# Keeping later chunks' q in block order through the MLP, with the stores putting rows in place and a new list of steps

**Chip, cores, metric.** One core of one Trainium2 chip. The metric is the device time of one execution in microseconds (us); lower is better.

## The reference, cut

```python
# attention: gated linear recurrence, B=4, H=8, S=768, D=48
state = alpha[:, :, t, :, None] * state + einsum('bhd,bhe->bhde', k[:, :, t], v[:, :, t])
y[:, :, t] = einsum('bhd,bhde->bhe', q[:, :, t], state)
# bridge to (3072, 384), then the MLP, d_ff = 2048
h = x @ w_in
g = h * np.clip(h + 3.0, 0.0, 6.0) / 6.0
out = g @ w_out
```

## The kernel before

24 chunks of 128 tokens (six for each batch) go through the recurrence; pairs of chunks ("groups") go through the MLP. The first six chunks are transposed by TensorE. From chunk 6 on (`FIRST = 6`) alpha, k and q are loaded in a layout from which VectorE's 32x32 block transposes make the columns; each transpose writes with a stride of four fp32, so that tokens come out in natural order:

```python
def by_blocks(to, name, j):
    nc.vector.transpose(out=to.rearrange("r p (u v) -> r p v u", v=V),
                        in_=quads[name, j % NQ][:, :, :, 0:BLK])
```

k must also be had with tokens in the partitions. From chunk 6 on it is turned by VectorE (`kt`), written to DRAM by four SyncE DMAs (`kw`), and read back by one (`kr`); TensorE uses it for the state update (`u`):

```python
def read_k(j):                                   # step kr
    kb_t[j] = wk.tile([C, NP, C], FP, tag="kb", name="kb")
    nc.sync.dma_start(out=kb_t[j].rearrange("s p r -> s (p r)"),
                      in_=far_t.pop(j).rearrange("s v p o c -> v s (p o c)"))
# ... cut: update(j), step u, multiplies kb_t[j] by v ...
def store2(g, i):                                # step O, on ScalarE's queue
    row, col = PLACES[i]
    j = G * g + row
    nc.scalar.dma_start(out=out[j * C : (j + 1) * C, col * HD : (col + 1) * HD],
                        in_=oh_t.pop((g, i)))
```

Loads, `kw` and `kr` all stand in SyncE's one queue, in order. The order on every engine is set by hand: a long list of words (`kw.12 ... lq.12 ... kr.12 ... u.12`), each word one step of one chunk or group. The framework adds the semaphores. (A semaphore marks that a piece of work is done; what depends on that work waits for it.) In the compiled program all DMAs of SyncE and ScalarE share eight completion semaphores in rotation, and a DMA of SyncE waits until the one that used its semaphore before has landed.

## Time and profile before

| | before |
|---|---|
| device time, first set of three | 568.94 us (568.49 to 569.09) |
| span of the profiled run | 564.6 us |
| first product of the second group (L692) | 113.2 us |
| first product of the last group | 543.2 us |
| last matmul | 561.2 us |

The prediction below shows the main lines. What TensorE waited for (total, times, longest, in us), and what SyncE's queue waited for, taken from the list of waits:

```profile
PE u_ps L410 <- DMA kb<-far: 2.1, 2, 1.1
PE tk_ps L288 <- DMA rings<-in_k_dram: 2.0, 2, 1.9
...
SPq L267 <- DMA out_dram<-oh: 27.7, 13, 4.6
```

The first line is the state update waiting for k's read-back. The last is SyncE, whose loads (L267) stood 13 times and for 27.7 us behind stores (`out_dram<-oh`) that they have no data in common with.

### The profile page before, as it was taken

The page shows a single profiled execution, that of the slowest core. Times are in us where ns is not written, and L with a number is a line of the kernel's source. Part 1 is how long each engine was busy: PE and PEld are TensorE (multiplying, and loading weights), DVE is VectorE, ACT ScalarE, POOL GpSimd, SP SyncE. Part 2 cuts the span into 40 slices and gives each one's busy share as a digit, 9 for nine tenths or more (in the row PEclk, how much of TensorE's full clock was granted, in tenths as well). Part 3 has the DMA queues.
Part 4 walks back from the last instruction along what each step waited for, and adds up shares of the span by engine and source line. Part 5 has one row for each costly group of instructions (what it writes and reads, how often), then busy time and mean ns, then how long its engine had stood idle before and what let it go on. Part 6 is the DMA issues. An engine that isn't in the chain of part 4 may idle for free.

```text
span 564.6 us, 12762 instructions
## 1 busy us (share of the span) xinstructions
PE 553.4 (98%) x5236; PEld 513.2 (91%) x5236; DVE 470.0 (83%) x798; ACT 196.4 (35%) x348; POOL 56.0 (10%) x70
## 2 busy tenths in 40 slices
PE   8899999999899999999999999999999999999997
PEld 7688987599799989999999999999999999999997
DVE  7866997999899999998998978976999967754580
ACT  1457664112332332322422422432521422432420
POOL 2333435200001000100000000000000000000000
PEclk9979999999999999999999999999999999999999
DMA  9999677103533636264264353153154340000000
GB/s 147 188 186 168 186 230 196 52 16 63 139 90 87 145 71 155 54 139 90 60 148 107 77 121 85 20 146 78 45 129 94 83 122 8 1 22 8 1 30 21
DMA packets 121272, 53.73 MB, mean 95 GB/s; under 512 B 80638, under 2 KB 114174, under 8 KB 121214
## 3 DMA queue, kind: packets, MB, share of 16 engines
q1 hardware_dynamic: 114588, 48.19, 40.8%
q10 hardware_dynamic: 6624, 4.72, 2.5%
q8 instruction: 41, 0.67, 0.5%
q14 instruction: 19, 0.14, 0.1%
HBM read 44.24 MB, written 8.65 MB: 94 GB/s over the span
## 4 chain that ended last, share of the span: by engine, by line
PE 89%; DMA 6%; DVE 2%; SPq 1%; issue 0%; ACT 0%; DVEq 0%; ACTq 0%
PE m_ps L692 35%; PE m_ps L592 29%; PE m_ps L471 6%; PE sc_ps L346 4%; PE m_ps L509 4%; PE y_ps L440 4%; DMA rings<-in_k_dram 3%; PE y_ps L450 2%; PE m_ps L482 2%; DMA t<-in_v_dram 2%; PE u_ps L410 2%; DMA kb<-far 1%; PE tk_ps L288 1%; DMA far<-kq 1%; PE m_ps L524 0%
## 5 line engine op out<-in xcount | busy, mean ns | idle before, releaser
L692 PE MATMUL m_ps<-w,g_sb 128*128 128x192 f32 x704 | 121.2, 328 | 0.0
L692 PEld LDWEIGHTS m_ps<-w,g_sb 128*128 128x128 f32 x704 | 113.8, 190 | 2.3 <-issue 1.4
L598 ACT COPY g_sb<-m_ps 128x512 f32<-128x512 f32 x110 | 64.3, 584 | 138.3 <-PE m_ps L592 123.9
L692 PE MATMUL m_ps<-rings,g_sb 128*128 128x192 f32 x528 | 91.2, 326 | 0.0
L692 PEld LDWEIGHTS m_ps<-rings,g_sb 128*128 128x128 f32 x528 | 85.7, 190 | 0.0
L592 PE MATMUL m_ps<-xc,w 128*128 128x128 f32 x640 | 83.2, 278 | 0.2 <-ACT g_sb L598 0.2
L592 PEld LDWEIGHTS m_ps<-xc,w 128*128 128x128 f32 x640 | 77.2, 192 | 3.3 <-issue 1.4
L487 ACT ACTIVATE r<-g_sb,half 128x512 f32<-128x512 f32 x80 | 55.5, 719 | 57.0 <-DVE g_sb L529 22.8
L491 DVE SCALAR_TENSOR_TENSOR g_sb<-r,g_sb 128x512 f32<-128x512 f32 x80 | 54.5, 700 | 8.1 <-PE m_ps L692 4.8
L397 POOL TENSOR_TENSOR t<-t,R 128x384 f32<-128x384 f32 x20 | 20.9, 1043 | 383.8 <-DVE t L425 206.0
L592 PE MATMUL m_ps<-xT,raw 128*128 128x128 f32 x400 | 51.8, 276 | 0.0
L592 PEld LDWEIGHTS m_ps<-xT,raw 128*128 128x128 f32 x400 | 48.7, 192 | 0.3
L529 DVE TENSOR_TENSOR g_sb<-m_ps,g_sb 128x512 f32<-128x512 f32 x30 | 20.5, 686 | 27.2 <-ACT g_sb L598 26.5
L592 PE MATMUL m_ps<-xT,w 128*128 128x128 f32 x320 | 41.9, 278 | 0.0
L639 DVE TENSOR_TENSOR g_sb<-g_sb 128x512 f32<-128x512 f32 (+1 forms) x55 | 41.7, 796 | 0.1
L592 PEld LDWEIGHTS m_ps<-xT,w 128*128 128x128 f32 x320 | 38.2, 192 | 1.2 <-issue 0.2
L352 DVE TENSOR_TENSOR A<-sc_ps,mask 128x512 f32<-128x512 f32 x48 | 30.8, 683 | 2.7 <-PE sc_ps L346 2.4
L592 PE MATMUL m_ps<-xc,raw 128*128 128x128 f32 x240 | 32.1, 277 | 0.7 <-ACT g_sb L598 0.7
L471 PE MATMUL m_ps<-xT,w 128*128 128x256 f32 x144 | 32.7, 381 | 0.0
L315 DVE TENSOR_TENSOR_SCAN R<-t,ones 128x516 f32<-128x516 f32 x24 | 29.3, 1223 | 3.1 <-ACT t L306 2.8
L529 DVE TENSOR_TENSOR g_sb<-g_sb 128x512 f32<-128x512 f32 x40 | 27.2, 683 | 5.5 <-ACT g_sb L598 5.4
L592 PEld LDWEIGHTS m_ps<-xc,raw 128*128 128x128 f32 x240 | 29.9, 192 | 1.2 <-ACT g_sb L598 0.9
(110 smaller groups left out, 711.4 us busy)
## 6 DMA issues: line engine op xcount, KB each, us to landing
raw<-in_moe_w_out_dram SPq DMA_DIRECT2D x8, 768.0 KB
t<-in_v_dram SPq DMA_DIRECT2D x48, 96.0 KB
raw<-in_moe_w_in_dram SPq DMA_DIRECT2D x24, 192.0 KB
out_dram<-oh ACTq DMA_DIRECT2D x44, 96.0 KB
far<-kq SPq DMA_DIRECT2D x60, 64.0 KB
kb<-far SPq DMA_DIRECT2D x15, 256.0 KB
kq<-in_k_dram SPq DMA_DIRECT2D x36, 96.0 KB
aq<-in_alpha_dram SPq DMA_DIRECT2D x36, 96.0 KB
```

The source lines that it names most:

```text
L315: nc.vector.tensor_tensor_scan(out=reverse(R, n - 1, n), data0=reverse(ax, n, n), data1=reverse(ones, n, n), initial=0.0, op0=ALU.mult, op ...
L346: nc.tensor.matmul(sc[h % 2][:, h // 2], K_t[j][r, h // 2], Q_t[j][r, h // 2], start=True, stop=True)
L352: nc.vector.tensor_tensor(out=A_t[j][:, NP * o : NP * (o + 1)], in0=ps_t.pop(("sc%d" % o, j)), in1=mask.unsqueeze(1).to_broadcast([C, NP, ...
L440: nc.tensor.matmul(y_of(j, (i + 1) // 2, p), vs[:, 2 * p + a, 32 * e : 32 * e + 32], A[:, NP * a + p], start=(i % 3 == 0), stop=(i > 1 and ...
L471: nc.tensor.matmul(h[:, f], w1[:, kk, o : o + C], xT_t[g][:, kk], start=(kk == 0), stop=(kk == KT - 1))
L487: nc.scalar.activation(out=to, in_=h, func=AF.Relu, bias=half, scale=1.0 / 6.0)
L491: nc.vector.scalar_tensor_tensor(out=to, in0=r, scalar=1.0, in1=h, op0=ALU.min, op1=ALU.mult)
L529: eng.tensor_tensor(out=out, in0=in0, in1=in1, op=ALU.add if s1 > 0 else ALU.subtract)
L592: nc.tensor.matmul(acc[g][i][:, f * C : (f + 1) * C], spots[w][:, f * C : (f + 1) * C], x_of(g, x), start=(first and f == 0), stop=last, s ...
L598: nc.scalar.copy(out=slots[z], in_=acc[g][i])
L639: nc.vector.tensor_tensor(out=out, in0=in0, in1=in1, op=ALU.subtract)
L692: nc.tensor.matmul(to[g], a, rhs[:, f], start=(first and f == 0), stop=(last and f == HF - 1), skip_group_check=True)
```

## The change

Intent: write q's transposes densely (cheaper for VectorE), carry the permuted token order through scores, state and MLP, and put rows right in the stores, for free. P, by which q is multiplied, is the running product of alpha; it stays in natural order and is now read with a stride of four. A second mask serves permuted columns. The list of steps was made anew.

```diff
+    mask4 = consts.tile([C, C], FP, tag="mask4")
+    nc.gpsimd.tensor_copy(out=mask4.rearrange("s (v u) -> s v u", v=4),
+                          in_=mask.rearrange("s (u v) -> s v u", v=4))
 ...
     def by_blocks(to, name, j):
-        nc.vector.transpose(out=to.rearrange("r p (u v) -> r p v u", v=V),
-                            in_=quads[name, j % NQ][:, :, :, 0:BLK])
+        nc.vector.transpose(out=fourth(to) if name != "q" else to.rearrange(
+            "r p (v u) -> r p v u", v=V), in_=quads[name, j % NQ][:, :, :, 0:BLK])
+    def fourth(t):
+        return t.rearrange("r p (u v) -> r p v u", v=V)
 ...
+        if name == "q" and j >= FIRST:
+            by = fourth(by)
+            to = src = t.rearrange("r p (v u) -> r p v u", v=V)
 ...
-                in1=mask.unsqueeze(1)...
+                in1=(mask if j < FIRST else mask4).unsqueeze(1)...
 ...
-        nc.scalar.dma_start(out=out[j * C : (j + 1) * C, col * HD : (col + 1) * HD],
-                            in_=oh_t.pop((g, i)))
+        to = out[j * C : (j + 1) * C, col * HD : (col + 1) * HD]
+        if j >= FIRST:
+            to = to.rearrange("(u v) n -> v u n", v=V)
+        nc.scalar.dma_start(out=to, in_=oh_t.pop((g, i)))
 ...
-        run("""la.0 z.3.5 lq.0 lk.0 lk.1 ta.0 la.1 ...
+        run("""la.0 z.3.5 la.1 lv.1.0 la.2 ta.0 lk.0 ...   (whole list new: 1651 words)
```

## The prediction

> **What bounds the kernel now.** I read the page's engine shares and slices first, then the stretches of 20 us, the groups with shapes kept apart, the waits, the timeline around the longest TensorE gaps and the last 25 us, and the transfer records.
>
> ```profile
> span 564.6 us, 12762 instructions
> PE 553.4 (98%) x5236; PEld 513.2 (91%) x5236; DVE 470.0 (83%) x798; ACT 196.4 (35%) x348; POOL 56.0 (10%) x70
> ...
> PE   8899999999899999999999999999999999999997
> ...
> DVE  7866997999899999998998978976999967754580
> ```
>
> TensorE is occupied in 98% of the span, VectorE in 83%, but in the slices from about 100 to 320 us VectorE is as full as TensorE. The stretches tell it in numbers (columns after the stretch: PE, PEld, DVE, ACT, POOL busy):
>
> ```profile
> 20.00:40.00 20.00, 18.09 (x234) 15.74 (x232) 14.03 (x22) 11.28 (x15) 6.11 (x5) 0.83 1.12 183
> ...
> 140.00:160.00 20.00, 18.05 (x229) 16.21 (x228) 18.31 (x30) 8.08 (x16) 1.24 (x1) 1.00 0.60 133
> 160.00:180.00 20.00, 20.00 (x151) 19.72 (x150) 19.92 (x39) 4.46 (x10) 0.00 (x0) 1.00 0.26 59
> ...
> 540.00:560.00 20.00, 20.00 (x128) 20.00 (x127) 9.96 (x17) 2.87 (x6) 0.00 (x0) 1.00 0.06 20
> ```
>
> "Busy" hides small stalls, so I took start-to-start intervals of the matmul records as well. In undisturbed runs a 128x192 product instruction takes 162.6 ns, a 128x128 one of the MLP 111.5 ns, a 128x256 one 216 ns, a 128x384 one about 325 ns. Each step priced at such a pace (15th percentile of its line) and summed over all 5236 instructions gives about 533 us. The first matmul starts at 1.5 us and the last ends near 561.5 us, so some 26 us lie above this floor: 12 in the first 40 us (3 of them because the granted clock was halved from 27.3 to 34.1 us), 1 from 40 to 120, 8 from 120 to 300, 4 to 5 after that. This 26 us is all that a change can win without removing TensorE work, and this one removes none.
>
> **What the Trainium skill says.** Three places.
> 1. "SBUF — State Buffer", section "Door 1: The DMA port swizzle": SBUF has 16-byte lines, and each access that crosses to another line pays, so fp32 can be strided by less than four for free. The trace agrees for writes: the two kinds of transpose below move the same 512 columns; the first writes with a stride of four fp32 (16 bytes), the second in contiguous runs of 32.
>
> ```profile
> L292 DVE STREAM_TRANSPOSE q<-qq 128x512 f32<-128x512 f32 x18 | 20.1, 1117 | 0.7 <-DMA qq<-in_q_dram 0.7
> ...
> L338 DVE TENSOR_TENSOR q<-q,P 128x512 f32<-128x512 f32 x18 | 12.4, 686 | 0.1
> ...
> L380 DVE STREAM_TRANSPOSE kq<-k 128x512 f32<-128x512 f32 x15 | 10.6, 706 | 0.1
> ```
>
> For a VectorE read with that stride no row of this trace tells.
> 2. "DMA: Bandwidth & Descriptors", section "Why a DMA increments its semaphore by 16 and not by 1": a copy runs on k of 16 DMA engines, k being the largest number up to 16 that divides the slowest dimension of both access patterns. The trace agrees: the read of the turned k, whose source is [4][32][512], ran 128 packets of 84 ns with 3.4 in flight on the mean in 4.8 us, while a store of [128][192] ran 128 packets of 36 ns with 10.7 in flight in 0.43 us.
> 3. "TensorE: Matmul & The Clock Gate", Part 1: the clock halves when TensorE has been idle for a window. The trace agrees: half clock from 27.3 to 34.1 us, after the idle stretch near 25 us (2.1 us waiting for chunk 2's k).
>
> **The change, part by part.**
> (a) *Transposes of q.* 18 chunks, now written contiguously: 1117 to about 706 ns by the third row above, 18 x 0.41 = 7.4 us less VectorE work, all of it after 110 us. VectorE isn't the bound; the gain is what of it reaches a TensorE wait.
> (b) *q times P.* P is now read with a stride of 16 bytes, in and out are contiguous. I choose "unchanged, 686 ns" at 0.65; otherwise up to about 1.1 us, which cancels (a).
> (c) *Masks.* A second mask for 18 chunks: the same operation in the same shape, 683 ns. Its building is one GpSimd copy of 128x128 early on, under 0.5 us, needed only at chunk 6: nothing.
> (d) *Scores, state, x, MLP.* Columns in another order; same shapes, same count. Nothing.
> (e) *Stores.* 36 of the 44 half-chunk stores (chunks from 6 on) go out to [4][32][192] instead of [128][192], the source stays [128]. Packets remain 128 of 768 bytes, but by place 2 on 4 DMA engines: 128 x 36 ns / 4 = 1.15 us instead of 0.43. [...]those take 0.55 to 0.65 us to issue (the kb read below), the store now 0.34. For 35 of them this is hidden; buffers are four deep. The last one ends the program:
>
> ```profile
> 561.58 0.32 ACT L705 COPY oh<-m_ps 128x192 f32<-128x192 f32 x1 [7.48 <-PE m_ps L692]
> 561.93 0.34 ACTq L713 DMA_DIRECT2D out_dram<-oh  x1
> ```
>
> Its packets ran from 562.77 to 563.20, the span ended at 564.6. So the end moves by 0.7 (transfer) plus 0.2 to 0.5 (issue): **+1.1 us**.
> (f) *Schedule, from chunk 6.* The compiled order of TensorE differs nearly everywhere. The two largest gaps of the middle are the first products with k read back through DRAM:
>
> ```profile
> 138.23 0.65 SPq L391 DMA_DIRECT2D kb<-far  x1
> ...
> 145.09 0.56 PE L410 MATMUL u_ps<-t,kb 128*48 128x48 f32 x16 [1.14 <-DMA kb<-far]
> ...
> 223.02 0.56 PE L410 MATMUL u_ps<-t,kb 128*48 128x48 f32 x16 [0.92 <-DMA kb<-far]
> ```
>
> Their gaps are 1.3 and 1.1 us above pace. The new order has 10 MLP products and two scores between the write of chunk 6's k and its use (10 x 0.89 + 2 x 1.1 = 11.1 us), the old one 9 and one (9.1 us), so the first goes. With these and part of the small waits on kept products, of 12 to 13 us I give back **2.5 us** (1 to 4).
> (g) *Schedule, start.* Old: chunk 0 first, then weights among the chunks. New: alphas 0 to 2 first, all inputs of chunks 0 to 2 before the first weights. Chunk 0's k goes from third to sixth place of the queue, at about 1.2 us for each 192 KB transfer some 2 to 3 us later; chunk 2's k comes before the weights instead of behind two slices. By 2.36 MB of inputs and 0.79 MB per slice at 150 to 190 GB/s the first slices would be there at about 20, 27, 31 and 37 us, against first uses at 19.8, 28.7, 35.7 and 42.0 before. The wait for chunk 2's k goes, and PE has more to do before 40 us. The warming matmuls stay 28. Of 12 us I give back **2 us**, between 0.5 lost and 4.5 won.
>
> Sum: -2.5 - 2.0 + 1.1 = -3.4 us; 568.9 - 3.4 = **565.5 us**, 0.6% faster.
>
> **Rivals.**
> *The VectorE relief pays in full.* All of (a) turns into time where both engines are full: another 3 to 5 us, about 561. For it: 19.9 of 20 us busy in several stretches. Against it: TensorE has only about 8 us of stalls there, mostly short, and some await transfers.
> *The strided read pays what the write saved.* (b) at 1.1 us: VectorE's sum is unchanged and the new order was made for a cost that isn't there; about 567 to 569. For it: place 1 doesn't set reads apart from writes. Against it: a change made for nothing else would hardly have stayed.
> *The stores on 4 engines hold back loads.* SyncE already waits 27.7 us, 13 times, for stores whose semaphores its loads share; three times longer stores lengthen that. About +1 us if it reaches k or v of a chunk, but there the DMA engines are under half busy.
> *The start goes wrong.* Later first scores, a longer idle stretch, another half-clock window: each 3.4 us of throttled work costs 1.7, so +2 to +3, about 569.
>
> **Range and chances.** Floor 533 + 1.5 + a tail of 4 is 539, but no schedule here comes near it; a change of 2% needs 11.4 us of 26, nearly half of all stalls, with the work unchanged: 0.05. Slower by 2% would need 11 us of new stalls in an order made with care: 0.02. Within: 0.93. The spread of (f) and (g) is some 2.5 us each way together with the rivals: 562 to 569.
>
> **What would show it right or wrong.** The q transposes at 0.70 to 0.73 us; q times P still 0.69 (rival two: over 1 us); VectorE's sum near 463 us; TensorE's busy time down by 2 to 5 us though its instructions are as many; the last store's packets spread over 1.1 to 1.3 us with four in flight and the time from the last copy to the end up by about 1 us; no TensorE gap over 1 us before chunk 6's update; first weight slices used by 37 us. I would be wrong if the start moved by over 4 us either way, if q times P were slow, or if the last store cost more than 2 us.

## The result and the profile after

| | before | after |
|---|---|---|
| device time | 568.72 us (4 runs) | 582.02 us (581.21 to 582.39, 4 runs) |
| ratio | 1 | 1.0231 (1.0214 to 1.0249) |
| span of the profiled run | 564.6 us | 580.6 us |
| first product of the second group | 113.2 us | 110.9 us |
| first product of the last group | 543.2 us | 558.0 us |
| last matmul | 561.2 us | 576.0 us |
| last matmul to the end | 3.4 us | 4.6 us |

A ratio here and below is from runs of the same rounds, so not quite the ratio of the medians quoted. The output is correct, and the kernel slower by 2.3%. The two profiled spans differ by 16.0 us, the timed medians by 13.3; the kernel before was between 564.4 and 570.1 us in all its later runs, so single spans are good to some 3 us only. Most of this scatter goes with the clock that TensorE was granted: of these 22 later runs the five with a mean clock of 0.999 or 1.0 took 564.4 to 566.9 us, the 17 with 0.990 to 0.997 took 567.3 to 570.1. A stretch at half clock is called a half-clock window below.

The span divides into three: the start gained 2.3 us (113.2 to 110.9, but see (g) below), the end lost 1.2 us, and the stretch from the first product of the second group to the first of the last went from 430.0 to 447.1 us, 17.1 more.

The page of the kernel after, engine shares and the clock's slices:

```profile
span 580.6 us, 12750 instructions
...
PE 557.1 (96%) x5236; PEld 513.7 (88%) x5236; DVE 475.7 (82%) x798; ACT 197.4 (34%) x348; POOL 53.8 (9%) x71
...
PEclk9999999999999999999999999999997999999999
```

TensorE runs the same 5236 instructions but is busy for a smaller share, and VectorE's sum has not fallen (470.0 before). The groups of VectorE tell why; they answer to the rows of q in the prediction:

```profile
L350 DVE TENSOR_TENSOR q<-q,P 128x512 f32<-128x512 f32 x18 | 19.5, 1081 | 0.1
...
L297 DVE STREAM_TRANSPOSE q<-qq 128x512 f32<-128x512 f32 x18 | 12.7, 706 | 1.7 <-DMA qq<-in_q_dram 1.6
```

The transposes fell from 1117 to 706 ns, and the product with P, which now reads with that stride, rose from 686 to 1081 ns: 18 x 0.411 = 7.4 us saved, 18 x 0.395 = 7.1 us paid. The rest of the rise of VectorE's sum came with the order: 474.4 us in the run with the old layout and the new list (e2 below).

The list of waits, TensorE's and SyncE's lines as above:

```profile
PE u_ps L422 <- DMA kb<-far: 9.1, 3, 4.5
...
SPq L271 <- DMA out_dram<-oh: 31.4, 13, 5.7
SPq L399 <- DMA out_dram<-oh: 7.1, 2, 4.8
```

The update of the state waits 9.1 us for k's read-back instead of 2.1. By start-to-start intervals of the matmul records there are four gaps before updates: 1.3 us (chunk 7), 1.3 (chunk 8), 3.6 (chunk 12), 4.7 (chunk 20) above pace, 10.9 us in all; before, two of 1.3 and 1.1 us. The granted clock was halved twice after such gaps, from 260.6 for 3.4 us and from 434.7 for 6.8 us; an estimate of its cost is half of the time in which TensorE had work there, some 4 to 5 us. These two account for about 13 of the 17 us; the rest is spread in small waits that I have not attributed.

What k's read-back itself waited for stands in the chain of waits of 236 to 262 us (kernel after; start, length, what):

```profile
244.11 5.41 PE m_ps L704 x32
249.52 0.02 issue
249.55 0.33 ACT oh L717
249.88 0.02 issue
249.90 3.18 DMA out_dram<-oh
253.08 0.02 issue
253.09 6.03 DMA kb<-far
259.12 0.04 issue
259.16 0.56 PE u_ps L422 x16
```

A product ends, ScalarE copies its result and issues the store at 249.90; the read-back of k is issued at 253.09, when that store has landed; the update starts at 259.16. The timeline of the same stretch shows what lies between:

```profile
242.34 2.59 SPq L399 DMA_DIRECT2D far<-kq  x4
...
244.97 7.48 SPq L271 DMA_DIRECT2D qq<-in_q_dram  x8
245.01 0.55 ACTq L728 DMA_DIRECT2D out_dram<-oh  x1
...
248.07 0.56 ACTq L728 DMA_DIRECT2D out_dram<-oh  x1
249.90 0.55 ACTq L728 DMA_DIRECT2D out_dram<-oh  x1
253.09 0.57 SPq L403 DMA_DIRECT2D kb<-far  x1
...
259.16 0.56 PE L422 MATMUL u_ps<-t,kb 128*48 128x48 f32 x16 [3.48 <-DMA kb<-far]
```

Eight loads of q, some 0.4 us each to issue, stand between k's write and its read-back and take 7.5 us, in good part because they wait for stores whose semaphores they are to reuse. The trace's records name the semaphores, and each wait ends within 0.03 us of the landing: the store of 245.01 (number 105) lands at 248.02, the load on 105 is issued at 248.04; the store of 248.07 (108) lands at 251.18, the load on 108 is issued at 251.20; the store of 249.90 (103) lands at 253.08, the read-back, on 103, is issued at 253.09.

The list of steps itself shows how much room there was. TensorE's work between two steps, priced (MLP product step 0.89 us, output product 2.6, scores 1.1 and so on):

| chunk | before: kw to u | before: kr to u | after: kw to u | after: kr to u |
|---|---|---|---|---|
| 6 | 9.1 | 4.5 | 11.1 | 3.8 |
| 7 | 10.5 | 6.1 | 11.2 | 3.5 |
| 8 | 12.5 | 4.4 | 12.8 | 3.8 |
| 12 | 24.3 | 15.8 | 12.1 | 2.7 |
| 13 | 25.0 | 18.9 | 14.7 | 4.3 |
| 20 | 28.5 | 19.7 | 10.5 | 4.4 |
| 21 | 33.4 | 27.4 | 25.1 | 6.1 |

From the issue of the read-back to its landing the trace has 6.0 us (253.09 to 259.12; the median of the 15 read-backs is 6.1). From chunk 12 on the old order left 15.8 to 27.4 us, the new order in six of ten chunks 2.7 to 6.1 (chunks 14, 15, 16, 18, 19 and 22, left out above, have 14.0, 10.3, 6.1, 25.4, 22.4 and 4.1). Little room alone did not make a long wait: before the updates of chunks 13 and 22 no gap was over 0.2 us. Between `kw` and `kr` of chunks 12 and 20, the two long waits, the new list has the loads of q of two chunks.

The end, kernel after (timeline; the same two lines of before are in the prediction):

```profile
576.36 0.32 ACT L717 COPY oh<-m_ps 128x192 f32<-128x192 f32 x1 [7.48 <-PE m_ps L704]
576.70 0.55 ACTq L728 DMA_DIRECT2D out_dram<-oh  x1
```

The store takes 0.55 us to issue instead of 0.34. By the transfer records its 128 packets start 1.19 us after the issue (0.84 before) and end 2.50 us after it (1.28 before): 1.31 us on four engines instead of 0.43 on sixteen.

### The profile page after: what moved, and what is told of

Read it like the earlier page. It is cut to its first block, busy times and chain, and to the rows that moved or that the text cites. A ratio compares the mean times of both kernels' runs of the same rounds, so it can differ in the third digit from the quotient of the medians.

```text
span 580.6 us, 12750 instructions
## 1 busy us (share of the span) xinstructions
PE 557.1 (96%) x5236; PEld 513.7 (88%) x5236; DVE 475.7 (82%) x798; ACT 197.4 (34%) x348; POOL 53.8 (9%) x71
## 4 chain that ended last, share of the span: by engine, by line
PE 77%; DMA 11%; DVE 7%; SPq 3%; issue 1%; ACT 0%; POOL 0%; ACTq 0%; DVEq 0%; POOLq 0%
PE m_ps L704 31%; PE m_ps L604 28%; PE m_ps L521 4%; PE m_ps L483 4%; PE sc_ps L358 3%; PE y_ps L452 3%; DMA kb<-far 3%; SPq L178 2%; DMA rings<-in_q_dram 2%; PE y_ps L462 2%; DMA out_dram<-oh 2%; DMA raw<-in_moe_w_in_dram 1%; PE u_ps L422 1%; DMA g_sb<-in_moe_w_in_dram 1%; DMA rings<-in_alpha_dram 1%
## 5 line engine op out<-in xcount | busy, mean ns | idle before, releaser
L704 PE MATMUL m_ps<-w,g_sb 128*128 128x192 f32 x704 | 124.5, 331 | 0.2 <-DVE g_sb L543 0.2
L704 PEld LDWEIGHTS m_ps<-w,g_sb 128*128 128x128 f32 x704 | 116.1, 193 | 1.7 <-issue 0.4
L704 PE MATMUL m_ps<-rings,g_sb 128*128 128x192 f32 x528 | 93.1, 330 | 0.0
L704 PEld LDWEIGHTS m_ps<-rings,g_sb 128*128 128x128 f32 x528 | 87.1, 193 | 0.3 <-DVE oh L720 0.2
L499 ACT ACTIVATE r<-g_sb,half 128x512 f32<-128x512 f32 x80 | 57.7, 723 | 76.3 <-DVE g_sb L503 24.4
L604 PE MATMUL m_ps<-xT,w 128*128 128x128 f32 x320 | 43.5, 281 | 0.0
L604 PEld LDWEIGHTS m_ps<-xT,w 128*128 128x128 f32 x320 | 38.6, 191 | 2.8 <-issue 2.0
L541 DVE TENSOR_TENSOR g_sb<-g_sb 128x512 f32<-128x512 f32 x40 | 27.4, 686 | 7.6 <-ACT g_sb L610 7.4
L483 PEld LDWEIGHTS m_ps<-xT,w 128*128 128x128 f32 x144 | 26.7, 190 | 5.3 <-POOL w L232 1.9
```

Source lines behind the costliest of these rows:

```text
L483: nc.tensor.matmul(h[:, f], w1[:, kk, o : o + C], xT_t[g][:, kk], start=(kk == 0), stop=(kk == KT - 1))
L499: nc.scalar.activation(out=to, in_=h, func=AF.Relu, bias=half, scale=1.0 / 6.0)
L541: eng.tensor_tensor(out=out, in0=in0, in1=in1, op=ALU.add if s1 > 0 else ALU.subtract)
L604: nc.tensor.matmul(acc[g][i][:, f * C : (f + 1) * C], spots[w][:, f * C : (f + 1) * C], x_of(g, x), start=(first and f == 0), stop=last, s ...
L704: nc.tensor.matmul(to[g], a, rhs[:, f], start=(first and f == 0), stop=(last and f == HF - 1), skip_group_check=True)
```

## The experiments

Theories before the runs. **S**: the slower form of the stores does it, in whatever order. **O**: the new order does it, as it puts k's read-back too late. **R**: VectorE's unsaved time does it. Times are medians of four runs; the kernel before was 567.5 to 568.7 us beside them.

| run | layout | order | stores on | time, us | ratio to before (95%) |
|---|---|---|---|---|---|
| before | old | old | ScalarE | 567.5 to 568.7 | 1 |
| after | new | new | ScalarE | 582.0 | 1.0231 (1.0214 to 1.0249) |
| e1 | new | old | ScalarE | 573.5 | 1.0081 (1.0032 to 1.0129) |
| e2 | old | new | ScalarE | 574.5 | 1.0107 (1.0070 to 1.0144) |
| e3 | new, plain stores | new | ScalarE | 575.8 | 1.0125 (1.0106 to 1.0145) |
| e5 | new, dense P | new | ScalarE | 579.4 | 1.0188 (1.0163 to 1.0213) |
| e6 | new | new, kr earlier | ScalarE | 581.2 | 1.0242 (1.0184 to 1.0301) |
| e7 | new, plain stores | old | ScalarE | 568.4 | 1.0038 (0.9974 to 1.0102) |
| e8 | new, plain stores, dense P | old | ScalarE | 568.9 | 1.0027 (0.9976 to 1.0078) |
| e9 | old | new start, then old | ScalarE | 566.2 | 0.9979 (0.9925 to 1.0032) |
| e13 | old | as e9, one kr earlier | ScalarE | 566.5 | 0.9993 (0.9941 to 1.0046) |
| e12 | old | old | GpSimd | 564.4 | 0.9947 (0.9891 to 1.0004) |
| e14 | old | new | GpSimd | 568.0 | 1.0015 (0.9979 to 1.0052) |
| e15 | new | old | GpSimd | 568.2 | 1.0008 (0.9960 to 1.0055) |
| e10 | new | new | GpSimd | 569.4 | 1.0042 (0.9984 to 1.0100) |
| e11 | old | as e9 | GpSimd | 563.4 | 0.9941 (0.9888 to 0.9994) |

(An e4, stores regrouped so that both sides divide by 16, was refused and has no run on record. "GpSimd" means all half-chunk stores but those of the last group.)

**Layout alone (e1).** The edit exchanges the list of steps only.

```diff
-        run("""la.0 z.3.5 la.1 lv.1.0 ...   (new list)
+        run("""la.0 z.3.5 lq.0 lk.0 ...     (old list)
```

> Edit: the changed kernel with the old list of steps: q in block order, second mask, reordered stores, but the schedule of before. Theory S (the stores on 4 DMA engines, landing 2.5 us after issue instead of 1.3, hold back SyncE's loads through shared semaphores whatever the order): 574 to 582 us. Theory O (it is the new order of steps, which queues the read-back of k behind loads that wait for late stores): the old order keeps its slack, so only the last store's 1.2 us shows and the time is 569 to 571 us. VectorE's sum is the same as before (about 470 us) under both, since the strided read costs what the transposes save.

573.5 us (570.0 to 575.0), between the theories: it decides neither. VectorE's sum is 471.1 us, as expected. The wait for chunk 10's k grew from 1.1 to 1.9 us and a half-clock window followed it; from chunk 12 on no update waited, as O says.

**Order alone (e2).** The old kernel with the new list.

> Edit: the kernel before with the new list of steps: natural order of q, plain stores on 16 engines. Theory S: about 565 to 568 us (the new order is good, and gains its 2.3 us of the start). Theory O: 576 to 581 us, TensorE still waits 1.3 to 4.7 us for the read-back of k at chunks 7, 8, 12 and 20, and the clock is halved after the long ones.

574.5 us: the order alone costs 5.8 us, below O's range and above S's. TensorE's list begins with

```profile
PE u_ps L410 <- DMA kb<-far: 5.3, 3, 3.1
```

Its gaps before updates were 1.0, 1.6 and 3.3 us at chunks 7, 12 and 20: the same places as after, smaller. Neither S nor O holds alone: order and layout cost 1.1% and 0.8%, together 2.3%.

**Plain stores in the new order (e3; wrong result).**

```diff
-        if j >= FIRST:
-            to = to.rearrange("(u v) n -> v u n", v=V)
```

> Edit: the changed kernel, but stores to [128][192] as before; the result is wrong on purpose (rows of chunks from 6 on stand in block order). Theory S: the waits for the read-back of k shrink to under 1 us each, 566 to 572 us. Theory O: 578 to 581 us, only the last 1.2 us and about 1 us per large wait come back. Either way the last copy to the end is 1.2 us shorter and a store takes 0.34 us to issue.

575.8 us: the form of the stores is worth 6 us in the new order, 1.2 of them at the end and so 4.8 before it. O's guess of 1 us per wait was too low, S's that the waits all but vanish too high: 2.1 and 3.6 us remained at chunks 12 and 20.

**Dense read of P in the new order (e5; wrong result).**

```diff
-            by = fourth(by)
-            to = src = t.rearrange("r p (v u) -> r p v u", v=V)
+            pass
```

> Edit: the changed kernel, but q times P reads P densely, in natural order; the result is wrong on purpose. The product of 512 columns should go from 1.08 back to 0.69 us and VectorE's sum fall by 7 us. Theory R (VectorE's unsaved 7 us is what made the kernel slow): 570 to 575 us. Theories S and O: 579 to 582 us, as VectorE isn't what the long waits wait for.

The product fell to 680 ns and VectorE's sum to 469.4 us. 579.4 us, a gain of 2.5 us by the ratios (1.0231 to 1.0188), at the edge of the scatter; theory R falls as the main cause.

**Read-back earlier (e6).** Four words of the new list moved ahead of the loads of alpha, v and q between `kw` and `kr`.

```diff
-... kw.12 ... lq.12 ... lq.13 ... kr.12 ... u.12
+... kw.12 ... kr.12 lq.12 ... lq.13 ... u.12      (kr.7, kr.8, kr.20 likewise)
```

> Edit: the changed kernel, complete and correct, with four steps moved in the list: the read-back of k of chunks 7, 8, 12 and 20 is issued ahead of the loads of alpha, v and q that stood between its write and it. Same work, same layout, same stores. Theory O (the read-back stands too late in SyncE's queue, behind loads that wait for stores): TensorE's four long waits (1.3, 1.3, 3.7 and 4.7 us) go or fall under 1 us each, and with them the two half-clock windows, so 568 to 574 us. If the read-back is late for want of DMA engines and not of its place in the queue: 579 to 582 us.

A miss: 581.2 us. The waits for k did go (from 9.1 to 0.3 us in the list of waits), but others came in their place, here TensorE's list in e6:

```profile
PE sc_ps L358 <- DVE q L350: 5.5, 2, 3.6
PE m_ps L704 <- ACT u L683: 2.1, 1, 2.1
```

and SyncE's:

```profile
SPq L271 <- DMA out_dram<-oh: 34.3, 11, 6.1
```

The eight loads of q, now behind the read-back, took 10.2 us to issue and chunk 13's scores waited for them; half-clock windows of 3.4 and 10.2 us followed the gaps. So O as I had it (one step misplaced) falls. New theory **W**: SyncE's queue as a whole is held up by stores through shared semaphores, and the new order has no room for that.

**Layout in the old order without its costs (e7, e8; wrong results).** The edits of e3, then of e3 and e5, on e1.

> Edit: the layout alone in the old order, with plain stores (rows of chunks from 6 on in block order, wrong on purpose). If the layout alone was 4.8 us slower because of the form of its stores: 567.5 to 570 us. If because of the order in which VectorE now has its shorter transposes and longer products: 572 to 574 us.

> Edit: as e7, and q times P reads P densely (wrong on purpose): what the layout would be worth if neither the stores nor the product cost anything, in the old order. VectorE's sum falls to about 463 us. By my prediction's step (a) some of the 7 us comes back: 565 to 568 us. If VectorE's time is hidden beside TensorE in this order: 568 to 570 us, as before.

With plain stores the layout costs nothing that these runs resolve (1.0038, against 1.0081 for e1; the intervals overlap). And with the product cheap as well, VectorE's sum is 464.1 us, six less than before, and the time is not better than before (1.0027). So in this order what the change set out to save was worth nothing that these runs resolve; a gain above some 0.25% (1.4 us) lies outside the interval. Both profiles have a longer gap before chunk 10's update (3.8 and 2.7 us start to start, 1.2 before) with a half-clock window behind it. Why is not shown, and it may hide a small gain.

**Hybrid (e9, e13).** Old layout; the new list up to the group-1 products, the old one from there, PSUM buffers renamed.

> Edit: the kernel before, natural order of q, with the new list of steps up to the first product of the second group (111 us) and the old list from there on, less the steps already done; PSUM buffers renamed so that no accumulation collides. If the new start is worth its 1 to 2.3 us and the loss lies after it: 566 to 568.5 us. If the start's gain is taken back by the first chunks after it: 568.5 to 570 us.

> Edit: the hybrid with the read-back of k of chunk 10 issued ahead of the v, k and q loads behind it. If only that read-back is late: its 2 us wait and the half-clock window after it go, 563 to 565.5 us. If the loads behind it then come late, as with the early read-backs in the new order: 566 to 568 us.

566.2 us; the start's gain is seen in the trace (109.8 us to the first product of the second group) but the time isn't resolved from before. e13, with 566.5 us, moved chunk 10's read-back earlier and, as in e6, the 2.2 us wait moved, from the update to a product after it: no gain.

**Stores on GpSimd (e10 to e12, e14, e15).** GpSimd's DMAs complete on semaphores of their own (111 to 118 in the trace), so no load shares one with them.

```diff
-        nc.scalar.dma_start(out=to, in_=oh_t.pop((g, i)))
+        (nc.scalar if g == NCH // G - 1 else nc.gpsimd).dma_start(out=to, in_=oh_t.pop((g, i)))
```

> Edit: the changed kernel with its half-chunk stores (all but the last group's) issued by GpSimd instead of ScalarE. In the compiled program the DMAs of SyncE and ScalarE share eight completion semaphores in rotation, and a load waits until the DMA that used its semaphore before has landed; GpSimd's DMAs have semaphores of their own. Theory W (after the early read-back, which only moved the wait to q: SyncE's queue as a whole is held up by waits for stores on shared semaphores, and the new order leaves no slack for it): SyncE's waits for out_dram (31 us over 13 waits, not counting the one at the end) disappear, TensorE's waits for k and q nearly too, 565 to 571 us. Theory B (the queue is short of transfer time, not held up): 577 to 583 us.

The changed kernel falls to 569.4 us: 11 us of the 13 by the ratios (1.0231 to 1.0042). Its stores land even later, as its table of DMA issues shows (the last column is the median us from issue to landing; the semaphore events of the kernel after give 2.8 for ScalarE's):

```profile
out_dram<-oh POOLq DMA_DIRECT2D x40, 96.0 KB, 3.6
```

So a late landing by itself is not what cost the 11 us. The loads' wait for stores (L271 for `out_dram<-oh`) is gone from SyncE's list, TensorE's list has

```profile
PE u_ps L422 <- DMA kb<-far: 1.2, 2, 0.8
PE u_ps L422 <- DMA kq<-in_k_dram: 1.0, 1, 1.0
```

and its granted clock is 1.0 over the whole span. W holds. Two things that the edit also changes do not explain it. The DMA engines were not freed: from issue to landing the 15 read-backs took 6.1 us at the median in the kernel after and 6.2 in e10, the 72 loads of q 2.6 in both; what changed is when they were issued. And ScalarE is spared 40 issues, but TensorE's list has only 1.3 us of waits for ScalarE's results in the kernel after and 1.0 in e10.

> Edit: the kernel before with its half-chunk stores issued by GpSimd. Theory W: its two waits for k (1.3 and 1.1 us) shrink, 565.5 to 568 us; its order has 15 to 27 us of TensorE work between read-back and use from chunk 12 on, so little else to win. Theory B: 568 to 570 us.

> Edit: the new order with the old layout (plain stores, natural q), its half-chunk stores issued by GpSimd. If the shared semaphores were the whole of what the new order costs (5.8 us with ScalarE's stores): as fast as the kernel before with GpSimd's stores or faster, 562 to 565.5 us. If the new order has a cost of its own (the read-back of k with 3 to 6 us of TensorE work before its use): 566 to 569 us.

> Edit: the old order with the new layout, its half-chunk stores issued by GpSimd (the last group's by ScalarE, in the 4-engine form). If the layout's cost in the old order (4.8 us) was the shared semaphores but for the last store: 564.5 to 566.5 us, the kernel before with GpSimd's stores and 1.2 us. If it was VectorE's longer product: 568 to 571 us.

With the coupling gone, against before with GpSimd's stores (0.9947), the order alone costs 0.7% (1.0015), the layout alone 0.6% (1.0008; 0.2% of it the last store, and its profiled run had a half-clock window in the start), both together 1.0% (1.0042). With the coupling both together cost 2.3%. So by the point estimates rather more than half of the loss is the coupling, and most of that arises where the order and the slow stores meet; each of these intervals is about half a per cent either way, so the split is not resolved further. e12 gained 0.5%, the upper edge of the interval just above 1. Its runs took 564.2 to 565.3 us, three of four at clock 1.0, where the kernel before, when it had that clock, took 564.4 to 566.9: what the old order paid for the sharing is not shown to be more than half-clock windows.

> Edit: the hybrid (old layout, new start, old list after it) with its half-chunk stores issued by GpSimd. Theory W: the 2 us wait at chunk 10 and its half-clock window go, 561 to 565 us. Theory B: 565 to 568 us, as the hybrid.

563.4 us (562.9 to 566.2), the lowest median, at 0.9941 (0.9888 to 0.9994): better than both kernels, though under 1% and not resolved from e12.

## Why the prediction was wrong

- **The step that failed is (f), "schedule, from chunk 6".** It gave back 2.5 us. The stretch lost 17 us in the profiled span (less by the timed runs, which lost 13.3 in all). I had read the two gaps that the kernel before shows, checked in the new list that chunk 6's was given more room (11.1 us from write to use against 9.1) and took that for the whole. Chunk 6 indeed did not wait (no gap over 0.25 us). But from chunk 12 on the old order kept 15 to 27 us of TensorE work between read-back and use, and the new one 2.7 to 6.1 in six of ten. The table above could be made from the two lists before any run. e2 shows that the order alone costs 1.1%, e10 that 11 of the 13 us go when the stores no longer share semaphores with the loads.
- **Rival three named the mechanism and missed its size.** "The stores on 4 engines hold back loads" through shared semaphores was put at +1 us, because the DMA engines are under half busy. That reading was itself off (the stretches of 20 us have shares up to 0.67 from 140 to 320 us), but their load was not what counted, as e10 shows: what was short was SyncE's queue, which stands still while one of its loads waits for a store. e3 puts the form of the stores at 6 us in the new order, e10 puts the coupling with its form and order together at about 11 us. I had SyncE's 27.7 us of such waits before me and took them for harmless, as in the old order they nearly were.
- **The waits were charged at their length only.** Gaps of over 2 us were in 16 of 19 cases followed by a half-clock window: after, 10.2 us at half clock behind two gaps. I counted that only for the start.
- **(a) was right, (b) wrong, and neither decided.** The transposes fell to 706 ns as said; the product rose to 1081 ns, the second rival's "up to about 1.1 us", to which I had given 0.35. But e8 shows no gain for VectorE's 6 us in the old order, and e5 some 2.5 us in the new. The sign that followed from (a), a VectorE sum near 463 us, failed (475.7), and so did TensorE's busy time: 2 to 5 us less was predicted, it rose by 3.7 (553.4 to 557.1).
- **(c) and (d) hold as far as seen:** the masked product stayed at 683 ns, and TensorE's instructions are as many.
- **(e) was right for the last store, wrong for the other 35.** At the end 1.2 us were measured, 1.1 predicted, by the terms named (issue 0.55 us, transfer 1.31 us on four engines). But "for 35 of them this is hidden" failed with (f): it looked at the buffers that a store frees and not at the semaphore that a load waits for, and e3 puts the form of the stores before the end at 4.8 us in the new order.
- **(g) was right in mechanism, and in size with some luck of the run:** 2.3 us gained in the start, 2 predicted. The 2.1 us gap near 23 us and the half-clock window behind it, which the kernel before has, are gone from the start. The ten profiles with the new start reach the second group's first product at 109.8 to 112.1 us. Of the six with the old start the four with that window reach it at 113.2 to 113.6, the two without (e7, e12; gaps of 1.7 and 1.9 us) at 110.6 and 111.2. So the gain is mainly the window, and the old start does not always have it.
- **The third place from the Trainium skill agrees only in part:** the half-clock window followed an idle stretch of 2.1 us, which is shorter than the window that the page means; see the last point of the list at the end.
- **The range and the chances** took it that an order "made with care" couldn't lose 11 us. That was a judgement of its making, not a reading of its order. That the order was made with a cheaper product and store in mind is likely, but was only argued.

Open: the 0.7% that the new order costs without the coupling, and some 4 us of small waits, are not attributed. e10's stores also differ in how they reach the DMA engines. Contention between stores and loads there is answered by the landing times under e10, and by the old layout with its 16-engine stores, which gained from GpSimd's stores too (e2 to e14: 1.0107 to 1.0015); no run gave ScalarE's stores semaphores of their own and left the rest as it was.

## What to carry to other kernels

When an order of steps changes, list for every transfer how much work of the bounding engine stands between its issue and its use, and compare it with the time to landing in the trace; one hand-off that looks better says nothing of the others. DMAs that share completion semaphores in rotation tie unrelated transfers together, so a slower store can hold up loads that the bounding engine needs; issuing the two from engines with separate semaphores took that away here. And moving time off VectorE, which stood beside the bound, won nothing that these runs resolve in the old order and some 2.5 us in the new; and as made, the change had only moved the strided access from the transpose to the product.

## What the Trainium skill lacked or had wrong

- "SBUF — State Buffer", section "Door 1: The DMA port swizzle", has the 16-byte line, but no cost for VectorE. Here both sides pay the same: a transpose of 512 fp32 columns writing with that stride took 1106 to 1129 ns in the kernels before and after against 706, a product reading one input with it 1081 against 686.
- "VectorE: DVE Perf Modes" says of the unpacked mode that strides "work" and gives no price; the product above is 1.58 times as long.
- "DMA: Bandwidth & Descriptors", section "Why a DMA increments its semaphore by 16 and not by 1": the rule for k holds for stores. It says nothing of the rest of the cost of a destination [4][32][192]: 0.55 us to issue against 0.34, first packet 1.19 us after the issue against 0.84.
- No page looked at tells of the framework's eight shared semaphores for SyncE's and ScalarE's DMAs, or that a load waits on them for stores: 31.4 us of SyncE's queue at its loads of alpha, k and q in the changed kernel, none there with GpSimd's stores.
- "TensorE: Matmul & The Clock Gate", "HAM oscillation", has the rule of no idle gaps over about 3.4 us. In the 16 profiled runs 19 start-to-start gaps between matmuls were over 2.0 us (2.06 to 4.9), and 16 of them were followed within 6 us by a half-clock window of 3.4, 6.8 or 10.2 us; the shortest were 2.06 us (e1, at 221.9, window from 225.3) and 2.13 us (before, at 23.4, window from 27.3). Three were not (e3: 2.2 us at 253.1, e5: 3.3 us at 254.1, e6: 2.3 us at 444.1). None of the gaps of 1.5 to 1.9 us was, and no window came without a gap before it.
